# Linear attention beside a routed feed-forward: eight rows added to the output by indirect DMA, feed-forward later, its weights behind the sweep

## The chip, the cores and the metric

The kernel runs on one core of one Trainium2 chip. The metric is device time in microseconds (us) of one execution; of several executions the median is taken. Before the change three runs gave 114.42 us as median (114.02 to 114.43).

## What is computed

```python
x  = A_x                                   # 2048 rows of 640, bf16
xn = layernorm(x)
out = x + A(xn) + B(xn)
# A: linear attention, 32 heads of 20
q, k, v = heads(xn @ wqkv)
pq, pk = phi(q), phi(k)                    # phi(t) = t + 1 if t > 0 else exp(t)
o = (pq @ (pk^T v)) / (pq @ sum(pk));  A = o @ wo
# B: a router picks the 8 best of 2048 rows
r = xn @ w_r;  idx = argsort(-r)[:8];  xs = xn[idx]
y = (silu(xs @ w_gate) * (xs @ w_up)) @ w_down * sigmoid(r[idx])
B = xn, with y added onto the 8 rows idx
```

So every row gets x + xn + attention, and eight rows, known only at run time, get y on top.

## The kernel before, in words

The 2048 rows are 16 tiles of 128. x_sb holds x, xn the normalized rows, xnT their transpose, pk and pqT the feature maps of k and of q (pqT transposed). The order of the work is written out by hand: each engine executes its instructions in the order of the program text, and every DMA stands in the queue of the engine that issues it (SP for nearly all, ACT for rd and every second output tile, POOL for the indirect one). SP is in order too: where one DMA waits for a semaphore, all later ones wait behind it.

**The sweep** (loop at L481) goes over the tiles. DVE takes statistics of tile t + 4 (stats2), POOL or ACT the root (root_pool L193, root_act L188), DVE normalizes (norm_dve L204), SP transposes tile t + 3 by DMA (tr_dma L237, called by turn L137), PE multiplies tile t with wk (k_half L242), ACT takes exp and relu (k_act L255), DVE forms pk (k_phi L266), PE adds to the Gram matrix (g1 L273). q is computed in 20 units u of 128 columns by 512 rows (q_mm L280, q_act L289, q_phi L296); units 0 to 7 lie in the sweep, the others later. turn(t) also issues weight loads by the table w_jobs (L131): wg behind the transposes of tiles 8 and 9, wu behind 11 and 13, and wv, wo and wd behind 15. POOL replaces x_sb by x + xn, tile by tile (adds L473), at the turns that add_at names; DVE does so for tiles 13 to 15 (L703). const_grep (turn 12, POOL) builds a constant of 32 partitions that copy_grep (L346, turn 13) copies to the three other quarters by DMA on SP.

**Behind the sweep**, load_s (L109) writes x + xn of all 16 tiles to the DRAM buffer s_dram, in three DMAs (L528, L529, L708). The router picks the eight rows; the row numbers go to idx_i, and POOL gathers the eight columns of xnT into xsT (L574). den (L583) computes the denominators of half of the rows. Those of half 0 take a trip through DRAM to be spread over the partitions: rden_out (L625, on ACT's queue) writes rd, rden_in (L631, two DMAs on SP) reads it back into spare, and rden_mul(j) (L637, DVE) multiplies 256 columns of pqT, the rows of output tiles 2j and 2j + 1. Those of half 1 are spread by PE (spread_mm, spread_copy, spread_mul) inside the output loop.

Then come the combined matrix of attention and wo (kv_mm, kv_out, m_unit), the gate and up matmuls for the eight rows (L730), q units 11 and 12, the down matmuls (L760), y8 (L768), an indirect DMA on POOL that adds y8 onto the eight rows of s_dram (L776), and four DMAs that read all of s_dram back into x_sb (L781). Then the q units up to 19, and **the output loop** (L846): o_mm (ten matmuls per tile), o_out (DVE adds x_sb, DMA to out), the last tile in three pieces (o_last).

Of the kernel before, what the change touches and what calls it, by code (L numbers as in the profile page):

```python
# [8 lines left out]
P = 128  # L9
S = 2048  # L10
D = 640
# [6 lines left out]
C = 8  # L18
# [5 lines left out]
QW = D // 4  # L24
EPS_BF16 = 1.0013580322265625e-05
NWARM = 6

BF16 = mybir.dt.bfloat16
F32 = mybir.dt.float32
# [7 lines left out]
def kernel(  # L37
# [26 lines left out]
    def sb(name, shape, dtype=BF16):  # L64
        return sm.tile(shape, dtype, tag=name, name=name)

    ps = psum.tile([P, 8, 512], F32, tag="ps", name="ps")
    rd = tc.dram_tile([4, D, 256], BF16, name="rd")
    s_dram = tc.dram_tile([S, D], BF16, name="s_dram")

    x_sb = big.tile([P, T, D], BF16, tag="x_sb", name="x_sb")
    xn = big.tile([P, T, D], BF16, tag="xn", name="xn")
# [33 lines left out]
    def kcw(w, src, lo, hi):  # L106
        SP.dma_start(w[:, lo:hi, :], src.rearrange("(kc p) n -> p kc n", p=P)[:, lo:hi, :])

    def load_s(a, b):  # L109
        SP.dma_start(  # L110
            s_dram[a * P : b * P, :].rearrange("(t p) d -> p t d", p=P), x_sb[:, a:b, :]
        )


# [9 lines left out]
    def load_cols(w, lo, hi, base):  # L124
        SP.dma_start(w[:, lo:hi, :], wqkv_v[:, lo:hi, base : base + D])

    def load_wd(lo, hi):
        SP.dma_start(wd[:, lo:hi, :], B_w_down.rearrange("(fc p) n -> p fc n", p=P)[:, lo:hi, :])


    w_jobs = {  # L131
        8: [lambda: kcw(wg, B_w_gate, 3, 5)], 9: [lambda: kcw(wg, B_w_gate, 0, 3)],
        11: [lambda: kcw(wu, B_w_up, 0, 3)], 13: [lambda: kcw(wu, B_w_up, 3, 5)],
        15: [lambda: load_cols(wv, 0, KC, 2 * D), load_wo, lambda: load_wd(0, 6), lambda: load_wd(6, FC)],
    }

    def turn(t):  # L137
        tr_dma(t)
        for job in w_jobs.pop(t, []):
            job()  # L140

    zw = sb("zw", [P, 512])
    V.memset(zw[:], 0.0)
# [93 lines left out]
    def tr_dma(t):  # L237
        nc.sync.dma_start_transpose(xnT[:, :, t * P : (t + 1) * P], xn[:, t, :])
# [41 lines left out]
    def q_mm(u, bank=7):  # L280
        tb, m = u // KC, u % KC
        for kc in range(KC):
            PE.matmul(  # L283
                ps[:, bank, :], lhsT=wq[:, kc, m * P : (m + 1) * P],
                rhs=xnT[:, kc, tb * 512 : (tb + 1) * 512],
                start=(kc == 0), stop=(kc == KC - 1),
            )
# [188 lines left out]
            add_s(i)  # L476

    q_at = {5: 3, 6: 4, 7: 5, 8: 6, 9: 7}
    add_at = {7: (0, 1), 9: (1, 1), 11: (2, 1), 12: (3, 2), 13: (5, 2), 14: (7, 3), 15: (10, 3)}
    later = {12: [const_grep], 13: [copy_grep]}  # L480
    for t in range(5, T):  # L481
        n = t + 4
        if 9 < n <= T:
            norm_dve(n - 1)
            turn(n - 1)
            shift(n - 1, 1)
        halves = (1, 0) if t == 5 else (0, 1)
        for b in halves:
            k_half(t, b)
        if n < T:  # L490
            stats2(n)
            if n % 2 == 0 or n < 12:
                root_pool(n)
        k_act(t, halves)
        if t == 5:
            root_act(8)
            norm_dve(8)
            turn(8)
            k_phi(4)
            q_phi(2)  # L500
        if t in q_at:
            q_mm(q_at[t])
            q_act(q_at[t])
        if t > 5:
            g1(t - 4)
        k_phi(t)
        if t in q_at:
            q_phi(q_at[t])
        if 11 < n < T and n % 2:
            root_act(n)  # L510
        for job in later.pop(t, []):
            job()
        if t == 5:
            shift(0, 9)
        if t in add_at:
            adds(*add_at[t])
# [8 lines left out]
                    start=(t == 0 and c in (0, 4)), stop=(t == T - 1), skip_group_check=True,  # L525
                )

    load_s(0, 8)  # L528
    load_s(8, 12)  # L529
    PE.transpose(psb[0:T, 1, 0:P], r_all[:], ident[:])  # L530
    g1(T - 4)
    r_row = sb("r_row", [T, P], F32)
# [23 lines left out]
    posf = sb("posf", [P, C], F32)  # L556
    junk = sb("junk", [P, P], F32)
    cols = sb("cols", [P, 3], F32)
    idx_i = sb("idx_i", [P, 1], I32)
    V.tensor_copy(allc[:, 0, :], ps[:, 1, 0:P])  # L560
    V.tensor_tensor(out=allc[:, 1, :], in0=ps[:, 1, P : 2 * P], in1=cst["iof"][:, P:], op=ALU.add)
    V.max(gv[:], allc[:, 0, :])
# [7 lines left out]
        out=junk[:], in0=cst["iof"][:, 0:P], scalar=cols[:, 0:1], in1=allc[:, 1, :],  # L570
        op0=ALU.is_equal, op1=ALU.mult, accum_out=cols[:, 1:2],
    )
    V.tensor_copy(idx_i[:], cols[:, 1:2])
    for c in range(C):  # L574
        at = G.value_load(idx_i[c : c + 1, 0:1], min_val=0, max_val=S - 1)
        G.tensor_copy(xsT[:, :, c : c + 1], xnT[:, :, bass.ds(at, 1)])
# [74 lines left out]
    def kv_out(b0, n, bank):  # L651
        V.tensor_tensor(
            out=kvz[0:EB, b0 * HB : (b0 + n) * HB].rearrange("p (g f) -> p g f", g=n),
            in0=ps[0:EB, bank, 0 : n * HB].rearrange("p (g f) -> p g f", g=n),
            in1=mask[:, b0 % 5 : b0 % 5 + n, :], op=ALU.mult,
        )

    def m_unit(m, b0, eng):
        for h in range(2):
            for i in range(2):  # L660
                b = 2 * m + i
                PE.matmul(
                    ps[HB * i : HB * (i + 1), b0 + h, 0:HW], lhsT=kvz[0:EB, b * HB : (b + 1) * HB],
                    rhs=wo[0:EB, b, h * HW : (h + 1) * HW], start=True, stop=True,
                    tile_position=(0, HB * i),
                )
        dst = Ms[:, m, :].rearrange("p (b f) -> p b f", b=2)
        eng(dst, ps[:, b0 : b0 + 2, 0:HW])
# [30 lines left out]
    V.reciprocal(gate[:, 2:3], gate[:, 1:2])  # L699
    V.tensor_copy(gateb[:], gate[:, 2:3])  # L700
    V.tensor_copy(gate[:, 2:3], gateb[:])
    V.tensor_scalar_add(rs1[:, 13:T], rs[:, 13:T], 1.0)
    for t in range(13, T):  # L703
        V.tensor_scalar(
            out=x_sb[:, t, :], in0=x_sb[:, t, :], scalar1=rs1[:, t : t + 1],
            scalar2=nm[:, t : t + 1], op0=ALU.mult, op1=ALU.add,
        )
    load_s(12, T)  # L708
    g2(range(0, T // 2), 2, 3)
    den(0, 6)  # L710
    rden_out()
# [12 lines left out]
    kv_mm(range(5, NB), 5)  # L724
    kv_out(0, 5, 4)
    kv_out(5, 5, 5)
    m_unit(0, 6, V.tensor_copy)
    m_unit(1, 2, A.copy)

    for a, w in enumerate((wg, wu)):  # L730
        for kc in range(KC):
            for j in range(4):
                PE.matmul(
                    ps[32 * j : 32 * j + 32, a, 0:FJ].rearrange("p (b f) -> p b f", f=32), lhsT=xsT[:, kc, :],
                    rhs=w[:, kc, :].rearrange("p (b j f) -> p j b f", j=4, f=32)[:, j],
                    start=(kc == 0), stop=(kc == KC - 1), tile_position=(0, 32 * j),
                )
    eg = late[:, 9:13, :].bitcast(F32).rearrange("p a b -> p (a b)")[:, 0 : 2 * FJ]
    eg = eg.rearrange("p (a b) -> p a b", a=2)
    ub = late[:, 5, 0:FJ]  # L740
    gu = late[:, 6, 0:FJ]
    hm = late[:, 7, 0:FJ]
    A.activation(eg[:, 0, :], ps[:, 0, 0:FJ], AF.Exp, scale=-1.0)
    V.tensor_scalar(
        out=eg[:, 1, :], in0=eg[:, 0, :], scalar1=1e30, scalar2=1.0, op0=ALU.min, op1=ALU.add
    )
    V.tensor_copy(ub, ps[:, 1, 0:FJ])
    V.tensor_tensor(out=gu, in0=ub, in1=ps[:, 0, 0:FJ], op=ALU.mult)
    m_unit(2, 6, V.tensor_copy)
    q_mm(11, 4)  # L750
    A.activation(eg[:, 0, :], eg[:, 1, :], AF.Ln)
    A.activation(eg[:, 1, :], eg[:, 0, :], AF.Exp, scale=-1.0)
    V.tensor_mul(hm, gu, eg[:, 1, :])
    hT = late[:, 8, 0:FJ]
    V.transpose(hT, hm)
    q_ev(11, 4)
    q_mm(12, 5)
    m_unit(3, 2, A.copy)
    q_act(12, 5)
    for fc in range(FC):  # L760
        for i in range(4):
            PE.matmul(
                ps[32 * i : 32 * i + 32, i % 2, 0:QW], lhsT=hT[:, 32 * fc : 32 * fc + 32],
                rhs=wd[:, fc, i * QW : (i + 1) * QW],
                start=(fc == 0), stop=(fc == FC - 1), tile_position=(0, 32 * i),
                skip_group_check=True,
            )
    y8 = sb("y8", [C, D])  # L768
    for i in range(4):
        y_o, y_i = y8[:, i * QW : (i + 1) * QW], ps[32 * i : 32 * i + C, i % 2, 0:QW]  # L770
        g_i = gate[32 * i : 32 * i + C, 2:3]
        if i % 2:
            V.tensor_scalar(out=y_o, in0=y_i, scalar1=g_i, scalar2=None, op0=ALU.mult)
        else:
            A.activation(y_o, y_i, AF.Identity, scale=g_i)
    G.indirect_dma_start(  # L776
        s_dram[:, :], bass.IndirectOffsetOnAxis(ap=idx_i[0:C, 0:1], axis=0), y8[:], None,
        compute_op=ALU.add,
    )
    for a in range(0, T, 4):  # L780
        SP.dma_start(  # L781
            x_sb[:, a : a + 4, :],
            s_dram[a * P : (a + 4) * P, :].rearrange("(t p) d -> p t d", p=P),
        )
    m_unit(4, 6, V.tensor_copy)
    q_phi(12)
    q_mm(13, 4)
    q_ev(13, 4)
    q_mm(14, 5)
    q_ev(14, 5)  # L790
    q_mm(15, 0)
    q_ev(15, 0)
    rden_mul(0)
    for u, b in ((16, 2), (17, 3), (18, 4), (19, 5)):
        q_mm(u, b)
        q_ev(u, b)
        if u == 16:
            rden_mul(1)

    def o_mm(t):  # L800
        b0 = 2 * (t % 2)
# [44 lines left out]
    for t in range(T - 1):  # L846
        o_mm(t)
        if t == 0:
            den(1, 4)
        if t in (1, 3, 5):  # L850
            spread_mm(1, H1[t // 2], 4)
            for i in range(2):
                spread_copy(1, H1[t // 2], 4, i)
        o_out(t)
        if t < 2:
            rden_mul(2 + t)
        if t in (2, 4, 6):
            for i in range(2):
                spread_mul(1, H1[t // 2 - 1], 4, i)
    o_last(T - 1)  # L860
# [1 line left out]
_INS = ['A_x', 'A_wqkv', 'A_wo', 'B_x', 'B_w_r', 'B_w_gate', 'B_w_up', 'B_w_down']  # L862
# [26 lines left out]
```

## Time and profile before

| | |
|---|---|
| median of 3 runs | 114.42 us |
| the profiled execution | 114.73 us |
| its span | 113.0 us |
| PE busy | 104.9 us, 906 matmuls |
| DVE, ACT, POOL busy | 80.7, 64.0, 38.7 us |
| granted TensorE clock | 1.0 in all slices |
| HBM read, written | 15.93 MB, 6.56 MB |

The profile is one execution; times in it count from the start of the span. A row of the timeline gives start, duration, engine, line, operation, output <- inputs, and in brackets how long the engine stood idle before it and what released it. PE's busy time is that of pipelined matmuls with modelled ends, so 93% busy doesn't mean that PE is at its peak. In the list of DMA issues the last figure is the median time from the issue to the landing. A row of the windows gives for a stretch the busy time of PE, PEld (weight loads), DVE, ACT and POOL with the number of instructions, then the granted clock, the mean busy share of the DMA engines and the GB/s that they moved.

### The profile page before, as it was taken

Reading aid. Unit: us, or ns where it says so; the run is one execution under the profiler, and the core shown is the slowest. Engines: PE = TensorE matmul, PEld = TensorE weight load, DVE = VectorE, ACT = ScalarE, POOL = GpSimd, SP = SyncE. Lnnn points to the kernel's source line nnn. Section 1 sums busy time; section 2 is a strip of 40 time slices with the busy share of each in tenths; the row PEclk is TensorE's granted clock in tenths of the full one; section 3 lists DMA queues with packets and bytes.
Section 4 is the critical chain, followed back from the end, with each engine's and each line's share of the span. In section 5 each row is a group of like instructions: output and inputs, shape, how many; then the busy total and the mean of one; then the engine's idle time right before and its main releaser. Section 6 shows DMA issues by size and latency. Waiting matters only on the chain.

```text
span 113.0 us, 2499 instructions
## 1 busy us (share of the span) xinstructions
PE 104.9 (93%) x906; PEld 62.0 (55%) x906; DVE 80.7 (71%) x182; ACT 64.0 (57%) x162; POOL 38.7 (34%) x85
## 2 busy tenths in 40 slices
PE   5689999999999895999999999999999999999970
PEld 2246645555555452655435979535445666677750
DVE  1798987999889897722719444697698887966660
ACT  1459996797687482666029454478996656100010
POOL 6904474031557529999960230000700000000000
PEclk9999999999999999999999999999999999999999
DMA  3998236895999997979999999929839982323332
GB/s 93 331 343 309 83 64 116 245 167 97 328 334 140 258 242 199 265 215 284 223 347 351 385 338 317 298 58 259 195 52 389 368 291 75 133 96 120 131 137 85
DMA packets 28007, 24.76 MB, mean 219 GB/s; under 512 B 8914, under 2 KB 26714, under 8 KB 27994
## 3 DMA queue, kind: packets, MB, share of 16 engines
q1 hardware_dynamic: 23808, 21.55, 68.9%
q10 hardware_dynamic: 4154, 3.03, 8.7%
q8 instruction: 7, 0.11, 0.4%
q14 instruction: 6, 0.05, 0.2%
q0 software_dynamic: 32, 0.01, 0.1%
HBM read 15.93 MB, written 6.56 MB: 199 GB/s over the span
## 4 chain that ended last, share of the span: by engine, by line
PE 55%; DVE 20%; DMA 8%; POOL 7%; issue 3%; ACT 2%; POOLq 0%; ACTq 0%
PE ps L804 16%; PE ps L283 12%; PE ps L275 8%; DVE stats L184 7%; DMA xnT<-xn 6%; PE ps L246 5%; DVE xn L205 4%; POOL rs L196 4%; PE ps L523 4%; POOL t L195 3%; DVE pk L268 3%; DVE pqT L299 2%; DVE mv L186 2%; DMA x_sb<-in_A_x_dram 2%; PE ps L645 2%
## 5 line engine op out<-in xcount | busy, mean ns | idle before, releaser
L246 PE MATMUL ps<-wk,xnT 128*128 128x320 bf16 (+1 forms) x160 | 24.9, 300 | 2.3 <-DMA xnT<-xn 1.9
L283 PE MATMUL ps<-xnT,wq 128*128 128x512 bf16 x100 | 23.6, 379 | 0.0
L804 PE MATMUL ps<-late,pqT 128*128 128x320 bf16 x150 | 21.4, 299 | 0.2 <-DVE o L813 0.2
L246 PEld LDWEIGHTS <-xnT 128*128 128x128 bf16 x160 | 14.9, 97 | 11.1 <-DMA xnT<-xn 3.2
L275 PE MATMUL ps<-pk,xn 128*128 128x512 bf16 x80 | 19.6, 379 | 0.0
L260 ACT ACTIVATE ek<-ps 128x320 bf16<-128x320 f32 x32 | 14.8, 461 | 5.9 <-PE ps L246 5.9
L804 PEld LDWEIGHTS <-pqT 128*128 128x128 bf16 x150 | 14.3, 98 | 6.6 <-issue 0.9
L299 DVE SCALAR_TENSOR_TENSOR pqT<-eq,rq 128x512 bf16<-128x512 bf16 x20 | 13.6, 685 | 4.7 <-ACT rq L293 4.7
L292 ACT ACTIVATE eq<-ps 128x512 bf16<-128x512 f32 x20 | 12.0, 598 | 8.4 <-PE ps L283 8.4
L268 DVE SCALAR_TENSOR_TENSOR pk<-ek,rk 128x640 bf16<-128x640 bf16 x16 | 12.8, 797 | 4.8 <-ACT rk L261 4.8
L813 DVE TENSOR_TENSOR o<-ps,x_sb 128x640 bf16<-128x640 f32 x15 | 12.3, 824 | 5.4 <-PE ps L804 4.6
L184 DVE BATCH_NORM_STATS2 stats<-x_sb 128x6 f32<-128x320 bf16 x32 | 14.4, 479 | 1.9 <-DMA x_sb<-in_A_x_dram 1.9
L283 PEld LDWEIGHTS <-wq 128*128 128x128 bf16 x100 | 9.4, 98 | 10.8 <-issue 0.7
L261 ACT ACTIVATE rk<-ps 128x320 bf16<-128x320 f32 x32 | 14.8, 461 | 0.0
L216 POOL TENSOR_SCALAR x_sb<-x_sb,rs,nm 128x640 bf16<-128x640 bf16 x13 | 13.3, 1034 | 0.7
L275 PEld LDWEIGHTS <-xn 128*128 128x128 bf16 x80 | 7.6, 98 | 8.1
L293 ACT ACTIVATE rq<-ps 128x512 bf16<-128x512 f32 x20 | 11.9, 593 | 0.0
L195 POOL TENSOR_SCALAR t<-mv 128x1 bf16<-128x1 f32 x10 | 4.8, 483 | 20.2 <-DVE mv L186 20.0
L205 DVE TENSOR_SCALAR xn<-x_sb,mv,rs 128x640 bf16<-128x640 bf16 x16 | 7.6, 476 | 4.3 <-POOL rs L196 3.7
L196 POOL TENSOR_TENSOR rs<-t,mhalf 128x1 f32<-128x1 bf16 x10 | 7.5, 749 | 0.8
L840 ACT CAST o<-ps 128x160 bf16<-128x160 f32 x1 | 0.3, 293 | 13.1 <-PE ps L830 13.1
L613 ACT CAST spare<-ps 128x1024 bf16<-128x1024 f32 (+1 forms) x6 | 4.9, 873 | 3.2 <-PE ps L599 3.2
(125 smaller groups left out, 100.6 us busy)
## 6 DMA issues: line engine op xcount, KB each, us to landing
x_sb<-s_dram SPq DMA_DIRECT2D x4, 640.0 KB, 6.2
wd<-in_B_w_down_dram SPq DMA_DIRECT2D x2, 960.0 KB
s_dram<-x_sb SPq DMA_DIRECT2D x1, 1280.0 KB, 11.7
s_dram<-x_sb SPq DMA_DIRECT2D x2, 640.0 KB, 8.2
rd<-rden ACTq DMA_DIRECT2D x1, 1280.0 KB
spare<-rd SPq DMA_DIRECT2D x2, 640.0 KB, 6.3
out_dram<-o SPq DMA_DIRECT2D x8, 160.0 KB, 1.8
wg<-in_B_w_gate_dram SPq DMA_DIRECT2D x1, 1152.0 KB, 7.5
```

The lines of the kernel that those rows point to most:

```text
L184: V.bn_stats(out=stats[:, t, b, :], in_=x_sb[:, t, b * HW : (b + 1) * HW])
L205: V.tensor_scalar(out=xn[:, t, :], in0=x_sb[:, t, :], scalar1=mv[:, t, 0:1], scalar2=rs[:, t : t + 1], op0=ALU.subtract, op1=ALU.mult,)
L216: G.tensor_scalar(out=x_sb[:, t, :], in0=x_sb[:, t, :], scalar1=rs1[:, sl], scalar2=nm[:, sl], op0=ALU.mult, op1=ALU.add,)
L246: PE.matmul(ps[:, b0 + b, 0:n], lhsT=xnT[:, kc, t * P : (t + 1) * P], rhs=wk[:, kc, b * HW : b * HW + n], start=(kc == 0), stop=(kc == KC ...
L260: A.activation(e[:, b, :], ps[:, b0 + b, 0:HW], AF.Exp)
L261: A.activation(r[:, b, :], ps[:, b0 + b, 0:HW], AF.Relu)
L268: V.scalar_tensor_tensor(out=pk[:, t, :].rearrange("p (b f) -> p b f", b=2), in0=e[:], scalar=1.0, in1=r[:], op0=ALU.min, op1=ALU.add,)
L275: PE.matmul(ps[:, 2 + c, :], lhsT=xn[:, t, c * P : (c + 1) * P], rhs=pk[:, t, 0:512], start=(t == 0), stop=(t == T - 1),)
L283: PE.matmul(ps[:, bank, :], lhsT=wq[:, kc, m * P : (m + 1) * P], rhs=xnT[:, kc, tb * 512 : (tb + 1) * 512], start=(kc == 0), stop=(kc == K ...
L299: V.scalar_tensor_tensor(out=pqT[:, m, tb * 512 : (tb + 1) * 512], in0=e[:], scalar=1.0, in1=r[:], op0=ALU.min, op1=ALU.add,)
L804: PE.matmul(ps[:, b0 + b, 0:HW], lhsT=pqT[:, kc, t * P : (t + 1) * P], rhs=Ms[:, kc, b * HW : (b + 1) * HW], start=(kc == 0), stop=(kc == ...
L813: V.tensor_tensor(out=o_t[:], in0=ps[:, b0 : b0 + 2, 0:HW], in1=x_sb[:, t, :].rearrange("p (b f) -> p b f", b=2), op=ALU.add,)
```

## The change

Tiles 0 to 10 no longer pass through s_dram: their x + xn stays in x_sb, and their share of the eight rows is added onto out itself by an indirect DMA once tile 10 is written. s_dram keeps tiles 11 to 15. Each of the two indirect DMAs skips the rows that the other one serves, by its bounds check; a second column of idx_i holds the row number less 1408, moved out of range for rows below 1408.

All weights but wk and wq are loaded behind the sweep. The feed-forward moves: gate and up behind q unit 13, down behind the last q unit, ahead of the output loop. The POOL adds and some evacuations change places.

```diff
+TS = 11
+NS = TS * P
-    s_dram = tc.dram_tile([S, D], BF16, name="s_dram")
+    s_dram = tc.dram_tile([S - NS, D], BF16, name="s_dram")
-    w_jobs = {
-        8: [lambda: kcw(wg, B_w_gate, 3, 5)], 9: [lambda: kcw(wg, B_w_gate, 0, 3)],
-        11: [lambda: kcw(wu, B_w_up, 0, 3)], 13: [lambda: kcw(wu, B_w_up, 3, 5)],
-        15: [lambda: load_cols(wv, 0, KC, 2 * D), load_wo, lambda: load_wd(0, 6), lambda: load_wd(6, FC)],
-    }
-    add_at = {7: (0, 1), 9: (1, 1), 11: (2, 1), 12: (3, 2), 13: (5, 2), 14: (7, 3), 15: (10, 3)}
+    add_at = {10: (0, 1), 11: (1, 1), 12: (2, 2), 13: (4, 3), 14: (7, 3), 15: (10, 3)}
-            turn(n - 1)
+            tr_dma(n - 1)
...
-    load_s(0, 8)
-    load_s(8, 12)
+    load_cols(wv, 0, KC, 2 * D)
+    load_wo()
+    for w, src in ((wg, B_w_gate), (wu, B_w_up)):
+        kcw(w, src, 0, KC)
+    load_wd(0, FC)
...
+    V.tensor_scalar(
+        out=gate[:, 0:1], in0=cols[:, 1:2], scalar1=float(NS), scalar2=float(2 * S),
+        op0=ALU.is_lt, op1=ALU.mult,
+    )
+    V.scalar_tensor_tensor(
+        out=gate[:, 1:2], in0=cols[:, 1:2], scalar=-float(NS), in1=gate[:, 0:1],
+        op0=ALU.add, op1=ALU.add,
+    )
+    V.tensor_copy(idx_i[:, 1:2], gate[:, 1:2])
...
-    load_s(12, T)
+    load_s(TS, T)
...
     m_unit(0, 6, V.tensor_copy)
     m_unit(1, 2, A.copy)
+    q_mm(11, 4)
+    q_ev(11, 4)
+    m_unit(2, 6, V.tensor_copy)
+    q_mm(12, 5)
+    m_unit(3, 2, V.tensor_copy)
+    q_ev(12, 5)
+    q_mm(13, 4)
+    q_act(13, 4)
+    gate_up()
...
+    m_unit(4, 6, V.tensor_copy)
+    q_mm(14, 5)
+    q_act(14, 5)
...
+    q_phi(14)
+    q_mm(15, 2)
+    q_ev(15, 2)
+    for u, b in ((16, 3), (17, 4), (18, 2), (19, 6)):
         q_mm(u, b)
         q_ev(u, b)
         if u == 16:
-            rden_mul(1)
+            rden_mul(0)
+    down()
+    for i in range(4):
+        y_o, y_i = y8[:, i * QW : (i + 1) * QW], ps[32 * i : 32 * i + C, 5 + 2 * (i % 2), 0:QW]
+        g_i = gate[32 * i : 32 * i + C, 2:3]
+        A.activation(y_o, y_i, AF.Identity, scale=g_i)
+    G.indirect_dma_start(
+        s_dram[:, :], bass.IndirectOffsetOnAxis(ap=idx_i[0:C, 1:2], axis=0), y8[:], None,
+        bounds_check=S - NS - 1, oob_is_err=False, compute_op=ALU.add,
+    )
-    for a in range(0, T, 4):
-        SP.dma_start(
-            x_sb[:, a : a + 4, :],
-            s_dram[a * P : (a + 4) * P, :].rearrange("(t p) d -> p t d", p=P),
-        )
...
         o_out(t)
-        if t < 2:
-            rden_mul(2 + t)
-        if t in (2, 4, 6):
+        if t == 4:
+            SP.dma_start(x_sb[:, TS:T, :], s_dram[:, :].rearrange("(t p) d -> p t d", p=P))
+        if t == TS - 1:
+            G.indirect_dma_start(
+                out[0, 0:NS, :], bass.IndirectOffsetOnAxis(ap=idx_i[0:C, 0:1], axis=0), y8[:], None,
+                bounds_check=NS - 1, oob_is_err=False, compute_op=ALU.add,
+            )
+        if t < 3:
+            rden_mul(1 + t)
+        if t in (3, 5, 6):
             for i in range(2):
-                spread_mul(1, H1[t // 2 - 1], 4, i)
+                spread_mul(1, H1[(t - 2) // 2 if t < 6 else 2], 4, i)
```

More of the change, by code (lines that the diff above doesn't have):

```diff
@@ L110, in load_s @@
         SP.dma_start(
-            s_dram[a * P : b * P, :].rearrange("(t p) d -> p t d", p=P), x_sb[:, a:b, :]
+            s_dram[a * P - NS : b * P - NS, :].rearrange("(t p) d -> p t d", p=P), x_sb[:, a:b, :]
         )
@@ L128, in load_wd @@
         SP.dma_start(wd[:, lo:hi, :], B_w_down.rearrange("(fc p) n -> p fc n", p=P)[:, lo:hi, :])
-    w_jobs = {
-        8: [lambda: kcw(wg, B_w_gate, 3, 5)], 9: [lambda: kcw(wg, B_w_gate, 0, 3)],
-        11: [lambda: kcw(wu, B_w_up, 0, 3)], 13: [lambda: kcw(wu, B_w_up, 3, 5)],
-        15: [lambda: load_cols(wv, 0, KC, 2 * D), load_wo, lambda: load_wd(0, 6), lambda: load_wd(6, FC)],
-    }
[L137 to L140, printed above, removed]
     zw = sb("zw", [P, 512])
@@ L497 @@
             norm_dve(8)
-            turn(8)
+            tr_dma(8)
             k_phi(4)
@@ L558 @@
     cols = sb("cols", [P, 3], F32)
-    idx_i = sb("idx_i", [P, 1], I32)
+    idx_i = sb("idx_i", [P, 2], I32)
     V.tensor_copy(allc[:, 0, :], ps[:, 1, 0:P])
@@ L572 @@
     )
-    V.tensor_copy(idx_i[:], cols[:, 1:2])
+    V.tensor_copy(idx_i[:, 0:1], cols[:, 1:2])
     for c in range(C):
@@ L726, with gate_up, down @@
     kv_out(5, 5, 5)
+    def gate_up():
+        for a, w in enumerate((wg, wu)):
+            for kc in range(KC):
+                for j in range(4):
+                    PE.matmul(
+                        ps[32 * j : 32 * j + 32, a, 0:FJ].rearrange("p (b f) -> p b f", f=32),
+                        lhsT=xsT[:, kc, :],
+                        rhs=w[:, kc, :].rearrange("p (b j f) -> p j b f", j=4, f=32)[:, j],
+                        start=(kc == 0), stop=(kc == KC - 1), tile_position=(0, 32 * j),
+                    )
+    def down():
+        for fc in range(FC):
+            for i in range(4):
+                PE.matmul(
+                    ps[32 * i : 32 * i + 32, 5 + 2 * (i % 2), 0:QW], lhsT=hT[:, 32 * fc : 32 * fc + 32],
+                    rhs=wd[:, fc, i * QW : (i + 1) * QW],
+                    start=(fc == 0), stop=(fc == FC - 1), tile_position=(0, 32 * i),
+                    skip_group_check=True,
+                )
     m_unit(0, 6, V.tensor_copy)
     m_unit(1, 2, A.copy)
[L730 to L736, printed above, removed]
-                )
+    q_mm(11, 4)
[6 more added lines that the diff above has]
+    q_act(13, 4)
     eg = late[:, 9:13, :].bitcast(F32).rearrange("p a b -> p (a b)")[:, 0 : 2 * FJ]
@@ L742 @@
     hm = late[:, 7, 0:FJ]
+    hT = late[:, 8, 0:FJ]
+    y8 = sb("y8", [C, D])
+    gate_up()
     A.activation(eg[:, 0, :], ps[:, 0, 0:FJ], AF.Exp, scale=-1.0)
@@ L746 @@
     )
+    A.activation(eg[:, 0, :], eg[:, 1, :], AF.Ln)
+    A.activation(eg[:, 1, :], eg[:, 0, :], AF.Exp, scale=-1.0)
+    q_phi(13)
     V.tensor_copy(ub, ps[:, 1, 0:FJ])
     V.tensor_tensor(out=gu, in0=ub, in1=ps[:, 0, 0:FJ], op=ALU.mult)
[L749 to L752, printed above, removed]
+    m_unit(4, 6, V.tensor_copy)
+    q_mm(14, 5)
+    q_act(14, 5)
     V.tensor_mul(hm, gu, eg[:, 1, :])
-    hT = late[:, 8, 0:FJ]
     V.transpose(hT, hm)
[L756 to L779, printed above, removed]
-    for a in range(0, T, 4):
-        SP.dma_start(
-            x_sb[:, a : a + 4, :],
-            s_dram[a * P : (a + 4) * P, :].rearrange("(t p) d -> p t d", p=P),
[L784 to L794, printed above, removed]
+    q_phi(14)
+    q_mm(15, 2)
+    q_ev(15, 2)
+    for u, b in ((16, 3), (17, 4), (18, 2), (19, 6)):
         q_mm(u, b)
@@ L797 @@
         if u == 16:
-            rden_mul(1)
+            rden_mul(0)
+    down()
+    for i in range(4):
+        y_o, y_i = y8[:, i * QW : (i + 1) * QW], ps[32 * i : 32 * i + C, 5 + 2 * (i % 2), 0:QW]
[4 more added lines that the diff above has]
+        bounds_check=S - NS - 1, oob_is_err=False, compute_op=ALU.add,
+    )
     def o_mm(t):
@@ L854 @@
         o_out(t)
-        if t < 2:
-            rden_mul(2 + t)
-        if t in (2, 4, 6):
+        if t == 4:
[4 more added lines that the diff above has]
+                bounds_check=NS - 1, oob_is_err=False, compute_op=ALU.add,
+            )
+        if t < 3:
+            rden_mul(1 + t)
+        if t in (3, 5, 6):
             for i in range(2):
-                spread_mul(1, H1[t // 2 - 1], 4, i)
+                spread_mul(1, H1[(t - 2) // 2 if t < 6 else 2], 4, i)
     o_last(T - 1)
```

## The prediction

> **What bounds the kernel now.** I read the page first, then the chain that ended last in order of time, then the waits, then the timeline and the windows of the places that the diff touches.
>
> ```profile
> span 113.0 us, 2499 instructions
> ```
> ```profile
> 37.68 6.47 DMA xnT<-xn
> ...
> 44.19 1.54 PE ps L246 x10
> ...
> 85.28 1.36 PE ps L804 x10
> ...
> 97.15 11.03 PE ps L804 x80
> ```
> ```profile
> SPq L632 <- DMA rd<-rden: 8.3, 1, 8.3
> ```
>
> The span is 113.0 us in an execution of 114.73, so 1.7 us lie around it. The median shown is 114.42, 0.3 below this execution: I sum against 114.73 and take 0.3 off at the end. Up to 44 us DVE, POOL and a late transpose set the end; from 44.19 PE runs nearly without a hole to the last tile. So the question is what can open a hole in PE after 44 us. Two things stand ready: transposes behind weight loads (the 6.47 us), and the round trip of rden through DRAM (L626 writes rd, L632 reads it back into spare, rden_mul at L639 uses it before the first output tile). SP waits 8.3 us in the middle of that trip, hidden today. The change lengthens the queue ahead of it.
>
> **The change part by part.**
>
> *1. Weights leave the sweep* (L107, two DMAs of wg and two of wu between the transposes on SP).
>
> ```profile
> PE ps L246 <- DMA xnT<-xn: 1.9, 2, 1.4
> ```
> ```profile
> DMA to landing us min/median/max: 2.6/3.7/6.6
> ```
> ```profile
> 44.88 0.20 ACT L191 ACTIVATE rs<-lg 128x1 f32<-128x1 f32 x1
> ...
> 45.42 0.43 ACT L261 ACTIVATE rk<-ps 128x320 bf16<-128x320 f32 x1
> ...
> 46.65 1.53 PE L246 MATMUL ps<-wk,xnT 128*128 128x320 bf16 x10
> ```
>
> The second row is that of L238: a transpose with nothing ahead of it lands in 2.6 us, one behind weights in up to 6.6. PE lost 1.9 us to this. Not all comes back, because ACT is late next: its root of tile 15 waits for DVE and ends at 45.08, and only then does ACT empty the bank of tile 12, whose first half is out at 45.85. Tile 13's matmuls, at 46.65 today, can't start much before 45.9. Gain in the sweep: **0.7 us**, ends 0 and 1.9.
>
> *2. Weights come behind the sweep, and start later.* On SP the three copies of grep now stand ahead of wv, and they wait for const_grep on POOL.
>
> ```profile
> 42.35 0.58 POOL L196 TENSOR_TENSOR rs<-t,mhalf 128x1 f32<-128x1 bf16 x1
> ...
> 43.34 0.90 POOL L216 TENSOR_SCALAR x_sb<-x_sb,rs,nm 128x640 bf16<-128x640 bf16 x1
> ```
> ```profile
> 45.85 0.71 POOL L341 TENSOR_SCALAR_AFFINE_SELECT grep<-grep 32x640 bf16<-32x640 bf16 x1
> ...
> 47.25 0.57 SPq L125 DMA_DIRECT2D wv<-in_A_wqkv_dram  x1
> ```
>
> The last root on POOL ends at 42.93 in both kernels (DVE sets it). Between it and const_grep stands one add (0.3 with its rs1, then 0.90); by the new add_at there are two. So grep ends at 46.56 + 1.25 = 47.8; three issues at about 0.6 each follow, and wv is issued near 49.8: **2.55 us later**.
>
> Then the bytes up to the landing of rd. Added: wg and wu, 3840 KB. Gone: s_dram of 11 tiles at 160 KB, 1760 KB. Net 2080 KB, 2.13 MB.
>
> ```profile
> 57.00:67.00 10.00, 10.00 (x159) 6.40 (x157) 5.64 (x25) 5.46 (x10) 2.78 (x8) 1.00 1.06 368
> 67.00:69.00 2.00, 2.00 (x42) 2.00 (x40) 0.69 (x1) 1.27 (x3) 0.41 (x2) 1.00 0.93 302
> 69.00:75.00 6.00, 6.00 (x106) 3.82 (x104) 3.77 (x8) 3.04 (x7) 0.00 (x0) 1.00 0.87 244
> 75.00:79.00 4.00, 3.98 (x67) 1.99 (x66) 3.31 (x8) 3.32 (x8) 0.00 (x0) 1.00 0.65 184
> ```
> ```profile
> 66.48 0.58 ACTq L626 DMA_DIRECT2D rd<-rden  x1
> ```
> ```profile
> 75.01 1.06 SPq L632 DMA_DIRECT2D spare<-rd  x2
> ```
>
> The last columns are the engines' DMA share and GB/s. While the DMA engines are full they move 368 GB/s, so 2.13 MB are **5.8 us**. Can a hole in today's queue take them? From 47 on the share is about 1; only 67 to 69 us shows a dip, (368 - 302) x 2 us = 0.13 MB, where SP waited for DVE before the last s_dram write. I give back 0.5 us for it. So rd, landed at 75.0 today, lands near 75.0 + 2.55 + 5.8 - 0.5 = **82.85**.
>
> That rd lands last, behind all of SP's loads, is an assumption that rests on these rows: rd is 1280 KB, 1.31 MB; from 69 to 75 us 244 x 6 = 1.46 MB moved. So nearly all of rd moved after 69, though issued at 66.48: it stood behind what SP had queued.
>
> The DMA page of the Trainium skill (DMA: Bandwidth & Descriptors, section Queues, rings and completion order) says that each DMA engine goes round its queues packet by packet, which would give rd a share from its issue on. The rows above show it late; they don't exclude a share by packets, since rd's rows are shorter than SP's. By the rule at equal shares the sum would be rival A's.
>
> The read-back: its first half is 640 KB, 0.655 MB; from 75 to 79 us 184 x 4 = 0.74 MB moved, so the first half was in by about 79.0, 4.0 us after its issue (upper end: 6.3, the row below). So spare is there at 82.85 + 4.0 = 86.85.
>
> ```profile
> spare<-rd SPq DMA_DIRECT2D x2, 640.0 KB, 6.3
> ```
> ```profile
> 82.73 0.82 DVE L639 TENSOR_TENSOR pqT<-pqT,spare 128x1280 bf16<-128x1280 bf16 x1
> ...
> 84.80 1.29 DVE L299 SCALAR_TENSOR_TENSOR pqT<-eq,rq 128x512 bf16<-128x512 bf16 x2
> ...
> 85.12 1.52 PE L804 MATMUL ps<-late,pqT 128*128 128x320 bf16 x10
> ```
>
> rden_mul(0) takes 0.82, so the first output tile starts at 87.7 instead of 85.12: **+2.6 us**. PE's own work up to there is the same 906 matmuls in another order; it would arrive at 85.12 - 0.7 = 84.4 and then stands 3.3 us. The 0.7 of the sweep is swallowed by this wait.
>
> *3. Behind the wait.* DVE is in order: the phi of units 17 to 19 stand behind rden_mul(0), 3 x 0.685, and den(1) needs the last of them, 2.05 us after the first output tile began; that tile keeps PE for only 1.37, so PE stands another 0.6. The loop also holds three rden_mul now instead of two (0.82 more on DVE). Up to tile 7 DVE then has 2.05 + 7 x 0.82 (L813) + 3 x 0.82 + six spread_mul, 3.3 (L620) = 13.6 us; PE today needs 97.15 + 1.37 - 85.12 = 13.4 for those 8 tiles. With DVE's unavoidable waits at the start I put 14.1: **+0.7 us** (ends 0 and 1.2).
>
> ```profile
> L299 DVE SCALAR_TENSOR_TENSOR pqT<-eq,rq 128x512 bf16<-128x512 bf16 x20 | 13.6, 685 | 4.7 <-ACT rq L293 4.7
> L813 DVE TENSOR_TENSOR o<-ps,x_sb 128x640 bf16<-128x640 f32 x15 | 12.3, 824 | 5.4 <-PE ps L804 4.6 <-issue 0.8
> L620 DVE TENSOR_TENSOR pqT<-pqT,spare 128x1024 bf16<-128x1024 bf16 (+1 forms) x6 | 3.3, 594 | 0.0
> ```
>
> *4. Costed at nothing.* wg and wu land near 70 to 72 by the same rates; the gate and up matmuls come at about 74 to 75, after q units 11 to 13. wd lands by about 79, down comes at 83. If wd were late it would only fill the wait for spare. The x_sb reload shrinks from 16 tiles to 5, first needed at tile 11. Three small DVE operations (0.15 each) stand before the x_sb updates at L704; load_s behind them has the whole weight queue as cover. y8 is all on ACT now, after down, inside PE's wait.
>
> The new wait at the end: POOL waits until the out writes of tiles 0 to 10 have landed, then adds eight rows to out. Nothing is queued behind it on POOL.
>
> ```profile
> 102.84 0.82 DVE L813 TENSOR_TENSOR o<-ps,x_sb 128x640 bf16<-128x640 f32 x1 [0.53 <-PE ps L804]
> ```
> ```profile
> out_dram<-o SPq DMA_DIRECT2D x8, 160.0 KB, 1.8
> ...
> s_dram<-y,idx_i POOLq DMA_INDIRECT x1, 3.4
> ```
>
> Tile 10's sum ends today at 103.66; + 3.3, + 1.8 landing, + 3.4 for the indirect DMA gives 112.2, against an end at 113.0 + 3.3 = 116.3. Cover 4 us; below zero only if the add on out takes over twice the 3.4.
>
> **Sum:** 2.6 + 0.7 = 3.3 us on 114.73, 118.0; less 0.3 for the median, **117.7 us**.
>
> **The rivals.**
>
> *A. rd shares the engines.* With half of 368 GB/s from about 67.5 on, rd is in by 75, and the read-back is issued early but stands in SP's queue behind wd and s_dram, which end when the same total has moved, 82.4. First half: 0.655 MB at 300 GB/s, 2.2 us: 84.6. First tile at 85.5, +0.4, with +0.7 of the loop: 115.5. For it: both queues use the same 16 engines. Against it: the windows from 69 on. Chance 0.15.
>
> *B. The read-back comes in time (not slower).* PE arrives at 84.4, so this decides at spare landed by 83.5, 3.35 us before my figure. It takes a full 368 GB/s or more through the slow stretch (47 to 57 us moves less today) and an earlier wv. Then the sweep's 0.7 stays, the third rden_mul of the loop takes back about half: 114.1; with all 1.9 us of the sweep returned, 113.1. For it: 3520 KB of s_dram traffic disappear in all, and the dip shows that today's queue is not quite full. Against it: half of it lay behind rd, where nothing waits. Chance 0.18.
>
> *C. Worse than the sum.* The read-back's first half takes the 6.3 us of its row, +2.3, or the slower 290 GB/s of all of 47 to 75 us holds for the added bytes (2.13 MB in 7.3 instead of 5.8 us, +1.5): 119.2 to 121. Chance 0.12.
>
> ```profile
> 47.00:75.00 28.00, 28.00 (x355) 17.61 (x354) 14.21 (x44) 14.28 (x34) 12.90 (x21) 1.00 0.99 290
> ```
>
> **How the numbers follow.** The forecast, a wait of 2 to 4.5 us at the first output tile (116.4 to 119.2), gets 0.55. The range leaves out the fast end of B and the far end of C: 114.0 to 120.0. A measurement of this kernel can tell about 0.5% (0.57 us) from no change. Faster by more: B with more than half of the sweep's other gain, 0.08. Within: the rest of B and the lowest part of A, 0.13. Slower: 0.79.
>
> **What would show it.** In the profile after: wv issued near 50; the wait of SP at L632's read-back for rd grown from 8.3 to about 16 us; DVE's rden_mul(0) near 86.9 with a DMA as its releaser; PE idle about 3 us before the first L804 group; no PE wait for transposes in the sweep, and tile 13's matmuls near 45.9. I am wrong if rden_mul(0) starts before 83.5, if the weights gate PE at gate and up (wu late), or if the chain ends in the indirect add on out.

## The result and the profile after

The changed kernel takes 117.81 us as median (before, measured beside it: 114.39). The ratio is 1.0296, 95% interval 1.026 to 1.0332: slower by 3 %. The prediction was 117.7. One of the four executions, at 119.66 us and the lowest clock of the four, is left out of the ratio as a slow one.

The profiled execution took 117.77 us with a span of 116.0, so the span grew by 3.0. (The median grew by 3.4; the profiled execution of before lay 0.3 above its median.) First the page of the kernel after: its span, and the granted clock in 40 slices.

```profile
span 116.0 us, 2489 instructions
PE 106.7 (92%) x897; PEld 62.6 (54%) x906; DVE 82.6 (71%) x184; ACT 64.0 (55%) x163; POOL 40.5 (35%) x85
...
PEclk9999999999999999999999999999996799999998
```

The clock line, in tenths of full clock, is what is new: 6 and 7 tenths in slices 31 and 32, where before had 9 throughout (9 stands for 90% or more). Next the chain of the kernel after that ended last, from tile 13's matmuls on (start, duration, what).

```profile
45.95 1.55 PE ps L236 x10
...
65.81 16.19 DMA rd<-rden
82.01 0.02 SPq L625
82.03 0.03 issue
82.06 4.53 DMA spare<-rd
86.59 0.02 issue
86.61 0.83 DVE pqT L632
87.45 0.05 issue
87.50 2.37 PE ps L806 x10
89.87 1.19 PE ps L580 x16
91.06 1.67 PE ps L806 x10
...
99.25 12.41 PE ps L806 x90
```

This is the whole story in order of time: the chain no longer runs through PE from 44 us to the end. It leaves PE at 64.8, passes two operations on ACT (not shown) and, from 65.81 on, the round trip of rden (16.19 + 4.53 us), then rden_mul(0) on DVE, and comes back to PE at 87.50 with the first output tile. In the chain before, that tile's row began at 85.28. The first row shows the sweep's gain: tile 13's matmuls at 45.95 instead of 46.65, released by ACT, no longer by a transpose. The rows from 87.50 on show a second loss: the first output tile takes 2.37 us. Before, its row in the timeline has 1.52 (the chain's 1.36 is shorter because it starts where the work ahead of it ends).

The waits of the kernel after confirm who waited (engine, line, waited for: us, times, longest):

```profile
DVE pqT L632 <- DMA spare<-rd: 4.2, 1, 4.2
...
PE ps L806 <- DVE pqT L632: 2.8, 1, 2.8
...
PE ps L236 <- ACT rk L251: 1.1, 2, 0.7
```

And the windows of the kernel after around that wait (busy us of PE, PEld, DVE, ACT, POOL, then granted clock, DMA share, GB/s):

```profile
83.00:85.00 2.00, 1.74 (x52) 0.99 (x50) 0.00 (x0) 2.00 (x5) 0.00 (x0) 1.00 0.76 209
85.00:87.00 2.00, 0.00 (x0) 0.00 (x0) 0.39 (x1) 1.33 (x4) 0.29 (x1) 1.00 1.18 314
87.00:89.00 2.00, 1.50 (x8) 1.00 (x9) 2.00 (x4) 0.00 (x0) 1.91 (x1) 0.76 0.55 132
89.00:91.00 2.00, 2.00 (x25) 0.79 (x23) 1.27 (x3) 0.00 (x0) 0.00 (x0) 0.50 0.06 10
91.00:93.00 2.00, 2.00 (x23) 1.09 (x20) 0.70 (x2) 0.89 (x2) 0.00 (x0) 0.89 0.24 82
```

PE is idle from 84.7 to 87.5; then its clock is granted at half while it works. If the clock was either full or half, the last three rows (0.76, 0.50, 0.89) add up to about 3.4 us at half: an estimate. The mean clock of the whole execution was 0.971 to 0.985 in all four executions of this kernel.

So the 3.0 us of the span are: the first output tile 2.22 later (87.50 - 85.28); from there to PE's last matmul 25.61 us (113.11 - 87.50) instead of 24.35 (109.63 - 85.28), 1.26 more; and the tail behind the last matmul 0.48 shorter (2.89 instead of 3.37). These are the chain's figures. The timeline has before's first output tile begin at 85.12, overlapping the work ahead of it; counted from there the first two terms are 2.38 and 1.10.

### The profile page after: what moved, and what is told of

Read it like the earlier page. It is cut to its first block, busy times and chain, and to the rows that moved or that the text cites. A ratio compares the mean times of both kernels' runs of the same rounds, so it can differ in the third digit from the quotient of the medians.

```text
span 116.0 us, 2489 instructions
## 1 busy us (share of the span) xinstructions
PE 106.7 (92%) x897; PEld 62.6 (54%) x906; DVE 82.6 (71%) x184; ACT 64.0 (55%) x163; POOL 40.5 (35%) x85
## 4 chain that ended last, share of the span: by engine, by line
PE 39%; DVE 23%; DMA 20%; POOL 8%; ACT 4%; issue 2%; POOLq 0%; ACTq 0%; SPq 0%
PE ps L806 19%; DMA rd<-rden 14%; DVE stats L174 9%; PE ps L265 7%; DVE xn L195 5%; POOL rs L186 5%; DMA spare<-rd 4%; PE ps L236 4%; POOL t L185 4%; DVE pqT L289 3%; DVE mv L176 3%; DVE pk L258 3%; DMA x_sb<-in_A_x_dram 2%; PE ps L513 2%; PE ps L273 2%
## 5 line engine op out<-in xcount | busy, mean ns | idle before, releaser
L806 PE MATMUL ps<-late,pqT 128*128 128x320 bf16 x150 | 22.4, 308 | 2.8 <-DVE pqT L632 2.8
L273 PE MATMUL ps<-xnT,wq 128*128 128x512 bf16 x93 | 23.0, 379 | 0.6 <-issue 0.3
L258 DVE SCALAR_TENSOR_TENSOR pk<-ek,rk 128x640 bf16<-128x640 bf16 x16 | 14.1, 879 | 3.7 <-ACT rk L251 3.7
L206 POOL TENSOR_SCALAR x_sb<-x_sb,rs,nm 128x640 bf16<-128x640 bf16 x13 | 12.8, 993 | 0.6
L797 POOL DMA_INDIRECT s_dram<-y,idx_i x1 | 2.2, 2200 | 19.5 <-ACT y L796 19.5
L860 POOL DMA_INDIRECT out_dram<-y,idx_i x1 | 1.4, 1356 | 21.5 <-DMA out_dram<-o 21.5
```

The lines of the kernel that those rows point to most:

```text
L206: G.tensor_scalar(out=x_sb[:, t, :], in0=x_sb[:, t, :], scalar1=rs1[:, sl], scalar2=nm[:, sl], op0=ALU.mult, op1=ALU.add,)
L258: V.scalar_tensor_tensor(out=pk[:, t, :].rearrange("p (b f) -> p b f", b=2), in0=e[:], scalar=1.0, in1=r[:], op0=ALU.min, op1=ALU.add,)
L273: PE.matmul(ps[:, bank, :], lhsT=wq[:, kc, m * P : (m + 1) * P], rhs=xnT[:, kc, tb * 512 : (tb + 1) * 512], start=(kc == 0), stop=(kc == K ...
L806: PE.matmul(ps[:, b0 + b, 0:HW], lhsT=pqT[:, kc, t * P : (t + 1) * P], rhs=Ms[:, kc, b * HW : (b + 1) * HW], start=(kc == 0), stop=(kc == ...
```

## The experiments

The theory: the loss is the read-back of rden, late because 3840 KB of weights stand ahead of it and start later, plus what PE's idle time does to its clock. The rival: the other parts (the late feed-forward, the two indirect adds, the new order of DVE's work) cost time of their own. The experiments were measured in two later rounds, in which before had medians of 114.72 (the first four) and 114.13 (the last three), so a difference between kernels of different rounds is uncertain by some 0.6 us; where it matters, the difference of the ratios to before is given too.

**Weights back in the sweep, the rest of the change kept.**

```diff
-            tr_dma(n - 1)
+            turn(n - 1)
...
-    load_cols(wv, 0, KC, 2 * D)
-    load_wo()
-    for w, src in ((wg, B_w_gate), (wu, B_w_up)):
-        kcw(w, src, 0, KC)
-    load_wd(0, FC)
```

> The kernel after, with the weight loads back at the sweep's turns 8, 9, 11, 13 and 15 as before; everything else of the change kept (s_dram of 5 tiles only, indirect add on out, feed-forward late). Theory (the whole loss is the read-back of rden, late because 3840 KB of weights stand before it and start later): 1760 KB less than before stand ahead of rd, so rd lands near 72 us, rden_mul(0) waits for no DMA, TensorE's clock stays at 1.0, and the time is 113.8 to 114.7. Rival (the other parts of the change, the late feed-forward and the two indirect adds, cost something of their own): 115.5 or more with no wait at rden_mul(0).

Measured: 114.86 us, ratio to before 1.0017 (0.9981 to 1.0053): no difference from before. The median lies 0.2 above my bound, and before had 114.72 in this round. In its chain the first output tile begins at 85.63:

```profile
84.68 0.94 PE ps L750 x48
85.63 1.47 PE ps L812 x10
...
95.74 12.41 PE ps L812 x90
```

No wait at rden_mul(0), no lower clock there. rd landed at 75.4, not near 72, which was still early enough: rden_mul(0) started at 83.21 without waiting for a DMA. Together, the other parts of the change neither cost nor gain anything measurable: the rival falls.

**Only the weights late, in the kernel before.**

```diff
+    load_cols(wv, 0, KC, 2 * D)
+    load_wo()
+    for w, src in ((wg, B_w_gate), (wu, B_w_up)):
+        kcw(w, src, 0, KC)
+    load_wd(0, FC)
     load_s(0, 8)
     load_s(8, 12)
```

> The kernel before with one edit: all weights behind the sweep, after the grep copies, ahead of the s_dram writes. Theory (bytes ahead of the read-back): 3840 KB more stand ahead of rd, 10.1 us at 380 GB/s, and the loads start 2.5 to 3.5 us later; so rd lands near 87 to 88 instead of 75 and spare 4.5 us later; rden_mul(0), at 82.7 today, moves to about 92, and the time to 122 to 125. Rival (the loss belongs to the new places of the feed-forward or the adds): under 117.

Measured: 121.73 us, ratio 1.0608 (1.0543 to 1.0672). A little below the range, in size and sign the theory's. In its chain:

```profile
52.85 24.27 DMA wd<-in_B_w_down_dram
...
77.16 1.01 PE ps L756 x48
...
83.70 5.24 DMA spare<-rd
...
88.97 0.82 DVE pqT L633
```

rd is there at 83.7 and not at 87, and rden_mul(0) starts at 88.97 instead of 92. The rate that I took, 380 GB/s, was right for the full stretch (375 GB/s from 70.0 to 83.7 us). What was wrong is that I put all added bytes behind before's 75 us: wv was issued 2.0 us later (49.27 instead of 47.25), and from there to rd's landing the mean is 340 GB/s, where before had 291, so part of the added bytes went where before's DMA engines moved less. The first rows show a second wait: as in the kernel before, the down matmuls stand early (76.21 there), and here PE waited 1.7 us for wd. Beside the kernel after, 117.81, this one is 3.9 us slower (3.6 by the ratios) with the same late weights: of the two kernels it is the one that still writes 11 tiles more to s_dram ahead of the read-back (the places of the feed-forward differ as well, and with them that wait for wd, so I don't put all of it on those bytes).

**No wait for the read-back.** The multiplication of the first half of the rows by their reciprocal denominators is done with values of xnT in place of spare, so this kernel leaves out the division there. All transfers stay.

```diff
-    V.tensor_tensor(out=sl, in0=sl, in1=spr[:, j * KC : (j + 1) * KC, :], op=ALU.mult)
+    V.tensor_tensor(out=sl, in0=sl, in1=xnT_f[:, j * KC : (j + 1) * KC, :], op=ALU.mult)
```

> The kernel after, but rden_mul multiplies by values of xnT, long resident, instead of spare: the division of the first half of the rows by their denominators is replaced by a meaningless factor. All DMAs stay. Theory: the wait at rden_mul(0) disappears, PE starts the first output tile near 84.8, the clock stays at 1.0, and the time is 113.6 to 114.6. Rival (order in the output loop, the third rden_mul on DVE, costs 0.7 us by itself as the prediction had it): 114.8 to 115.5.

Measured: 113.26 us, ratio 0.9867 (0.9807 to 0.9928). Even below the range: with this one wait gone the changed kernel is 4.5 us faster (117.81 to 113.26; 4.9 by the ratios) and beats the kernel before. The third rden_mul in the output loop costs nothing that shows: from the first output tile to the last matmul it is 23.98 us (108.68 - 84.70), before 24.35. So the rival of this run falls too. In its chain:

```profile
84.70 1.46 PE ps L808 x10
86.16 0.66 PE ps L580 x20
```

**PE kept busy during the wait.** Twelve matmuls of zeros into a free bank.

```diff
     down()
+    warm(12, 0)
     for i in range(4):
```

> The kernel after with 12 matmuls of zeros into a free bank between the down matmuls and the first output tile: about 2.6 us of PE work that waits for nothing, so that PE doesn't stand idle while rden_mul(0) waits for spare. The wait itself stays. Theory (behind the wait the loss is the lower granted clock, 0.5 in 89 to 91 us): the first output tile takes 1.4 instead of 2.4 us, clock 1.0 throughout, time down by 1.0 to 1.5. Rival (behind the wait DVE binds, the phi of units 17 to 19 and a third rden_mul, as predicted): the clock stays at 1.0 too, but the time falls by 0.5 or less, and den(1) waits for DVE.

Measured: 116.09 us, 1.7 below the kernel after (ratio to before 1.0112, 1.005 to 1.0174; the kernel after has 1.0296, so 2.1 by the ratios). That is more than the 1.0 to 1.5 that I gave it. The wait is the same, the work behind it isn't. Its chain:

```profile
65.77 16.35 DMA rd<-rden
...
82.17 4.46 DMA spare<-rd
...
86.65 0.87 DVE pqT L632
...
87.57 1.53 PE ps L807 x10
89.10 0.66 PE ps L580 x20
89.76 1.47 PE ps L807 x10
...
97.75 12.41 PE ps L807 x90
```

The first output tile starts at 87.57 as before the filling, but takes 1.53 us, den(1) 0.66 instead of 1.19, and the page shows the clock at 9 in all slices. From the first output tile to the last matmul it is 24.05 us (111.62 - 87.57). So behind the wait the clock was the loss, about 1.6 us (25.61 - 24.05), and DVE, with the same work in both, was none.

**Loads started earlier:** the grep copies behind the weight loads.

```diff
-    later = {12: [const_grep], 13: [copy_grep]}
+    later = {12: [const_grep]}
...
     load_wd(0, FC)
+    copy_grep()
```

> The kernel after with one edit: the three grep copies are issued behind the weight loads, so that wv no longer waits for POOL's const_grep. Theory (start and bytes add up): wv is issued near 47.2 instead of 50.72, so rd lands 3.4 us earlier, near 78.6, spare near 83.1, PE comes at 84.7 and hardly waits, the clock stays at 1.0: 113.2 to 114.2. Rival (the landing of rd is set by its small packets beside the large ones, not by the start of the loads): rd lands after 80.5, PE still waits over 1 us, 115 or more.

Measured: 113.80 us, ratio 0.9967 (0.9936 to 0.9997). The chain still passes the read-back, but only just:

```profile
79.07 4.64 DMA spare<-rd
...
83.73 0.84 DVE pqT L633
...
84.62 1.53 PE ps L807 x10
```

wv was issued at 46.79 instead of 50.72, and the read-back at 79.07 instead of 82.06. That is worth 4.0 us of time (3.8 by the ratios): the first output tile begins 2.9 earlier, and from there to the last matmul it is 24.05 us instead of 25.61, with the clock at 9 in all slices; the tail is 0.5 longer.

**As that, and the s_dram write behind the read-back.**

```diff
-    load_s(TS, T)
...
     for j in (0, 2):
         rden_in(j)
+    load_s(TS, T)
```

> As the kernel after, with the grep copies behind the weight loads and also the s_dram write of tiles 11 to 15 behind the two read-back DMAs of rd. Theory: 800 KB less stand before the read-back, 2.2 us, so rd lands near 76.5 and spare near 81; no wait at rden_mul(0): 113.0 to 113.6, faster than both kernels and as fast as the run without the read-back wait (113.26). Rival (taking the write away leaves the DMA engines idle while SP waits for rd, and the late s_dram write delays the indirect add and the reload of x_sb): the last tiles wait for x_sb, over 114.

Measured: 113.33 us, ratio 0.9924 (0.99 to 0.9949), faster than both kernels and equal to the kernel without the wait. rd landed at 77.0, and rden_mul(0) started at 82.28 without waiting for a DMA. Its chain has no DMA left from 45 us on:

```profile
83.75 0.94 PE ps L745 x48
84.70 1.46 PE ps L807 x10
```

**As that, and wd behind the read-back too.**

```diff
     for w, src in ((wg, B_w_gate), (wu, B_w_up)):
         kcw(w, src, 0, KC)
-    load_wd(0, FC)
     copy_grep()
...
         rden_in(j)
+    load_wd(0, FC)
     load_s(TS, T)
```

> As the run before, with wd (1920 KB) too behind the read-back. Theory (the DMA engines are the bound of this stretch, whatever the order): rd lands near 72.5 and spare near 77, but wd then lands near 84, so the down matmuls at 82.8 wait for wd about 1 us and the gain is smaller: 113.6 to 114.6. Rival (only rd's place in the queue matters): as fast as the run with wd ahead, 113.0 to 113.6.

Measured: 115.30 us, ratio 1.0091 (1.0058 to 1.0124), a miss by 0.7 above the range. Its profile is of the longest of its executions (117.41 us), so I read the order in it and the DMA traffic up to wd's landing: rd lands at 72.7, and wd at 86.2.

```profile
65.94 6.77 DMA rd<-rden
...
73.88 12.30 DMA wd<-in_B_w_down_dram
...
86.22 1.79 PE ps L745 x41
```

Now the down matmuls wait for wd. Moving one transfer ahead made another the late one: wd stands behind the whole wait of SP for rd and behind both read-backs. It lands 2 us after the 84 that I worked out, and the theory of a full DMA stretch is what failed: in the page's slices of 2.9 us the engines moved 231, 240 and 79 GB/s from 66.5 to 75.2, against 367, 354 and 326 GB/s from 67.0 to 75.3 in the run before. With wd behind the read-back, rd went alone, and then SP had to see it landed and issue the read-back before wd could start.

## Why the prediction was right, point by point

**1. The sweep.** Forecast 0.7 us, tile 13 near 45.9: it began at 45.95, and the release by ACT is in the waits. Right, and swallowed by the wait as said; in the kernel without the wait, tile 13's matmuls began at 45.92 and the first output tile at 84.70 instead of 85.28.

**2. Start and bytes.** The start was mis-sized: wv was issued at 50.72, 3.5 us later than before and not 2.55. The second add on POOL took 1.63 us instead of 0.90 (why was not tried), the last root on POOL ended 0.2 later, and the building of grep took 0.1 longer.

```profile
44.69 1.63 POOL L206 TENSOR_SCALAR x_sb<-x_sb,rs,nm 128x640 bf16<-128x640 bf16 x1
...
50.72 0.58 SPq L127 DMA_DIRECT2D wv<-in_A_wqkv_dram  x1
```

Against that, the bytes took 1.8 us less than the 5.3 of the sum. These are windows of the kernel after, two with wg and wu in flight, one with rd beside wd.

```profile
63.00:65.00 2.00, 1.84 (x41) 1.56 (x40) 1.78 (x10) 0.21 (x2) 0.56 (x4) 1.00 1.03 397
65.00:67.00 2.00, 2.00 (x27) 1.53 (x26) 1.06 (x3) 1.25 (x4) 0.55 (x3) 1.00 1.03 401
...
73.00:75.00 2.00, 2.00 (x12) 0.55 (x10) 1.92 (x3) 1.13 (x3) 0.00 (x0) 1.00 1.09 380
```

Before, rd had gone nearly alone from 69 to 73 us at about 300 GB/s; here its bytes moved beside SP's in a stream of 380. From wv's issue to rd's landing the mean was 320 GB/s instead of 291. The two errors cancel, by luck: rd landed at 82.0 where 82.85 was forecast. The read-back took 4.53 for its first half and not 4.0; rden_mul(0) started at 86.61 (86.85 forecast), the first tile at 87.50 (87.7), 2.38 later than the 85.12 on which the forecast of 2.6 was counted.

**Why rd lands last.** I had it stand behind all that SP had queued. For most of its time that was wrong as a mechanism. The DMA queues of the kernel after from 72 to 76 us (packets, MB, share of the 16 engines):

```profile
q1 hardware_dynamic: 853, 1.09, 73.0%
q10 hardware_dynamic: 851, 0.44, 35.9%
```

q1 is SP's, q10 ACT's, which carries rd. They take turns packet by packet, 853 to 851. That DMA engines go round their queues packet by packet is what the Trainium skill says in DMA: Bandwidth & Descriptors, section Queues, rings and completion order. The trace agrees with taking turns; its packets are single rows, while the page's packet holds several descriptors, and that grouping these counts can't show. But rd's packets are 512 bytes and SP's, wd and then s_dram, 1280, so taking turns gives rd 0.44 of 1.53 MB, 29 %. Ahead of that rd moved next to nothing for 4 us (65.81 to 69.9). Together, it lands about as late as if it had waited. In the kernel before, the rows of the prediction were read rightly: nothing of rd moved from 66.5 to 69, and from 69 to 71.5 it had 1207 packets beside 125 of SP's, with SP's queue nearly empty by then. With the longer queue of the kernel after the same rule no longer held. Rival A had the right rule, but with equal bytes instead of equal packets, and with a start at 67.5.

**3. Behind the wait.** This step failed. Forecast +0.7 because DVE would bind (three phi and a third rden_mul); measured +1.26 (1.10 by the timeline), and none of it DVE's: with PE kept busy the loop takes 24.05 us, less than the 24.35 of before, with the same DVE work as in the kernel after. PE's clock, which the sum put at nothing, cost about 1.6. That the term had the right sign was luck.

**4. Costed at nothing.** It held: the first experiment puts the rest of the change at 1.0017. The add on out starts at 110.41 and lands 3.0 us later, at 113.4, 2.6 us before the end of the span (4 forecast); POOL's long wait for it had cover.

```profile
out_dram<-y,idx_i POOLq DMA_INDIRECT x1, 3.0
```

Not forecast: the tail is 0.48 us shorter. Why was not tried; over the nine profiles of this document it lies between 2.9 and 3.8 us.

So 117.7 beside 117.81 is in part luck. By the timeline's counts the wait was forecast 0.2 too long, the loop 0.4 too short and for another reason, and the tail's 0.48 was not in the sum. The sum on the profiled execution was 3.3 where 3.0 was measured, and the 0.3 taken off for the median hid that: the profiled execution of the kernel after lies at its median.

The rivals: B (the read-back in time) is what the kernel without the wait and the one with the s_dram write behind the read-back made true. It gives 113.3, faster than the 114.1 that I allowed it with the sweep's 0.7 alone, since the output loop (24.0 instead of 24.35 us) and the tail (2.9 instead of 3.37) are shorter too.

## What to carry to other kernels

Before moving loads off a stretch where they disturb, add up the bytes that a later transfer on the same queue then has ahead of it, and the time at which the first of them can start; a round trip through DRAM stays hidden only if the queue ahead of it is short enough. The right repair was not to undo the move but to order the queue by due time: start the loads before what waits for another engine, and put writes that nobody needs soon behind the transfer that somebody does. Moving wd behind it as well went too far: then wd was the late one. If PE must wait a few us, filling the hole with matmuls that wait for nothing can pay (1.7 us here), because the work behind the hole then runs at full clock.

## What the runs showed of the hardware

An idle stretch of PE of 2.8 us (84.7 to 87.5) was enough for the granted clock to fall to 0.5 from about 88 to 91; filled with matmuls, it stayed at 1.0. The Trainium skill (TensorE: Matmul & The Clock Gate, section HAM oscillation — how this bites in real kernels) warns of gaps above about 3.4 us; here a shorter one did it, so the measurement stands against that bound. In the kernel with the grep copies behind the loads, where PE hardly waited, the mean clock was 0.998.

Two DMA queues share the engines by packets, not by bytes: a transfer with short rows gets the smaller part of the bytes beside one with long rows (0.44 beside 1.09 MB, at 851 and 853 packets).

rd, issued at 65.81, moved next to nothing before 69.9, while SP's queue moved about 400 GB/s. Rows of 3072 bytes (wu) ran then, but they are not needed for it: with the grep copies behind the loads rd was issued at 65.6 and moved nothing before 70, beside packets of 1.3 KB on average. With SP's queue empty at its issue, in the run with the weights back in the sweep, rd was moving by 68.0 after an issue at 66.70. What held it stays open.
